# Filler products in TensorE's queue while batch 0 is being prepared

## The chip, the core and the metric

The kernel runs on one core of a Trainium2 chip. The metric is the device time of one execution in microseconds (us), as the median of several executions. A profile is taken of one execution more; it lists what every engine did, and the TensorE clock that was granted in each stretch (1.00 is 2.4 GHz, 0.50 is 1.2 GHz).

## What is computed

For each of 4 batches of 12480 rows of 128 numbers, 32 inducing rows attend to the batch (giving `h`, 32 x 128), then the batch attends to `h`, and a two-layer network with a squared ReLU follows:

```
h = mab(I, x)                      # softmax(scale * I x^T) x, 32 x 128 per batch
y = mab(x, h)                      # softmax(scale * x h^T) h, 12480 x 128 per batch
r = maximum(y @ w_in, 0)           # 128 -> 2048
out = (r * r) @ w_out              # 2048 -> 128
```

## The kernel before

Since every row of `y` is a mixture of the 32 rows of `h`, the kernel does not multiply rows by `w_in` at all. For each batch it works out, once, weights on squares of pairs of attention weights (`w16`, four blocks of 128 x 128, made from products `G_0` to `G_3`), on single squares (`side`) and a linear part (`lin`). Then it streams the batch in 26 chunks of 480 columns: `ups` makes the differences of pairs on TensorE (tile `hp`), `lifts` squares them on ScalarE (`g`), `downs` multiplies by the weights on TensorE (`po`), `evictions` and `stores` write the result.

The program has two parts. Until about 52 us it loads the weights and makes `h` of batch 0 in program order (`first`). From there on an own list scheduler, `Order`, decides the order. Each stage of the kernel is a generator that yields one operation at a time: its engine, an assumed duration, a due time and what it needs. `Order.run` keeps an assumed clock per engine; it finds the earliest possible start of any waiting operation, and of those that could start on that engine within `PATIENCE` (0.159 us) it takes the one with the earliest due time. So what is written here is an order per engine, fixed when the program is built. On the chip each engine works through its own queue in that order, waiting where an input has not come.

Between `h` of batch 0 and the first `downs` lie three strands that the prediction follows:

- `readings`: for each of 7 groups G the scores of batch 0 against `h` (L419, tile `s`, operands `xp` and `hT`; four 32-row products beside each other, fp32), read out of PSUM by VectorE (L791, tile `scored`). One PSUM tile, the ring `att`, serves all scores, so the next scores wait for VectorE's reading. `attention` makes the softmax from them on VectorE, GpSimd and ScalarE (among it L820 on VectorE and L823 on GpSimd, tile `a`) and stores it to DRAM (`ad`); `squares` loads it back as `dT`.
- `first_softmax`: the scores of batch 1 against the inducing rows (L419 again, operands `xp` and `indT_sb`), read by VectorE at L675 (tile `sT`), through the same ring `att`.
- `prepare` and `pair_weights`: the weights of batch 0. TensorE's products into the tile `bank` (L902, L948, L952, L967, L982 to L987, L1009), VectorE's steps between them (L958 to L961 on `pl`, `inc`, `hot`; L989 to L1000), VectorE's `G_0` to `G_3` (L1060), and TensorE's four blocks of pair weights (L1076, tile `wq`), each evicted by ScalarE. `mark("wq", b, c)` is set when block c has been placed in the order. The first `downs` needs the fourth block.

In the names of the orders below, `s_0_3` are the scores of batch 0, group 3 against `h`; `s_1_3` those of batch 1, group 3 against the inducing rows. The PSUM pool `ps_o` has two buffers, and the ring `po_ring` stands for them.

Of the kernel before, what the change touches and what calls it, by code (L numbers as in the profile page):

```python
# [9 lines left out]
F32 = mybir.dt.float32  # L10
# [8 lines left out]
P = 128  # L19
NB = 4  # L20
MI = 32
# [4 lines left out]
CH = 4 * TP  # L26
# [4 lines left out]
NQ = 4  # L31
# [148 lines left out]
def op(engines, took, due, *needs, alone=False, hold=None):  # L180
    return engines, took, due, needs, alone, hold
# [3 lines left out]
def attend_then_relu2_mlp(ctx: ExitStack, tc: tile.TileContext, xn, xT, indT, w_in, w_out, outT):  # L185
# [19 lines left out]
    nc = tc.nc  # L205
# [418 lines left out]
    def mark(*key):  # L624
        return marks.setdefault(key, Mark())
# [12 lines left out]
    def x_loads():  # L638

        for b in range(1, NB):  # L640
            for G, w in enumerate(WID):
                end = yield op("SP1", 3.0 * w / CH, h_due(b) - X_AT - 2.0 * (NG - G), xp_ring, alone=True, hold=HOLD)
                xp_ring.held.append(mark("read", b, G))
                sts[b].xp[G] = load_xT(b, G, flow, NX)
                mark("x", b, G).t = end

    def row_loads():

        for b in range(1, NB):
            for h in range(HALVES):  # L650
                i = h % XB
                end = yield op("SP1" if h < HALVES - 1 else "SP5", 1.5, h_due(b) - ROWS_AT + ROWS_STEP * h, xnb_free[i], alone=True, hold=HOLD)
                sts[b].rows[h] = load_half(b, h, xnb[i])
                xnb_free[i] = mark("used", b, h)
                mark("rows", b, h).t = end
# [113 lines left out]
    def readings():  # L769

        for b in range(NB):
            st = sts[b]
            for G in range(NG):
                w, t = WID[G], BLK[G]
                wb = 32 * t
                X = nominal(NCH * b + 4 * G) - 14 - SLACK
                due = X - READ_AT
                if b < NB - 1:
                    due = min(due, h_due(b + 1) - READ_UNTIL - READ_STEP * (NG - G))
                end = yield op("PE", 0.83, due, att, mark("h", b))  # L780
                done = att.take()
                ps = att_psum(f"s2_{b}_{G}")
                scores(ps, st.hT, st.xp.pop(G), w)
                mark("read", b, G).t = end
                end = yield op("DVE", 0.62, due + 1, slots)
                gone = slots.take()
                k = 480 * ((NG * b + G) % SLOTS)
                e = scored[:, k:k + 480].rearrange("p (t i) -> p t i", i=MI)
                if wb > w:
                    nc.vector.memset(ps[:, w:wb], 0.0)  # L790
                nc.vector.transpose(e.rearrange("p t i -> p (t i)")[:, 0:wb], ps[:, 0:wb])  # L791
                done.t = end
                order.add(attention(b, G, e, X, end, gone))

    def attention(b, G, e, X, since, gone):
# [40 lines left out]
        done.t = end  # L836
        mark("ad", b, G).t = end

    def squares():

        for b in range(NB):
            st = sts[b]
            for G, n in enumerate(GRP):
                X = nominal(NCH * b + 4 * G) - 11 - SLACK
                rows = slice(0, MI * n)
                end = yield op("SP3", 1.4, X, mark("ad", b, G), dT_ring, alone=True)
                dT_ring.held.append(mark("over", b, G))
                dT = st.aT[G] = load_dT(b, G)
                mark("dT", b, G).t = end
                order.add(square(b, G, n, X, rows, dT))  # L850
# [236 lines left out]
    def ups():  # L1087

        for n, (b, c) in enumerate(CHUNKS):
            st = sts[b]  # L1090
            for j in (0, 1):
                end = yield op("PE", 0.21, nominal(n - 1.5 + UP_STEP * j), hp_ring, mark("dT", b, c // 4), alone=True)
                hp_ring.held.append(mark("lifted", n, j))
                dT = st.aT[c // 4][:, :, (c % 4) * TP:(c % 4 + 1) * TP]
                hp = hps[n, j] = two_banks(f"hp_{b}_{c}_{j}")
                for i in range(2):
                    nc.tensor.matmul(  # L1097
                        hp[:, i, 0:CH].rearrange("p (q t) -> p q t", q=4), pairs[half(i), (2 * j + i) * P:(2 * j + i + 1) * P],
                        dT[half(i)], start=True, stop=True,
                    )  # L1100
                mark("up", n, j).t = end

    def lifts():

        for n, (b, c) in enumerate(CHUNKS):
            for j in (0, 1):
                end = yield op("ACT", 0.92, nominal(n - 1 + j / 2), mark("up", n, j), *([] if j else [g_ring]), alone=True)
                if j == 0:
                    g_ring.held.append(mark("down", n))
                    gs[n] = mlp.tile([P, NQ, CH], F16, tag="g", name=f"g_{b}_{c}")  # L1110
                nc.scalar.activation(gs[n][:, 2 * j:2 * j + 2], hps.pop((n, j))[:, 0:2, 0:CH], AF.Square)  # L1111
                mark("lifted", n, j).t = end
            mark("g", n).t = end

    def downs():

        for n, (b, c) in enumerate(CHUNKS):
            st = sts[b]
            needs = [mark("g", n), mark("zz", b, c // 4), mark("wq", b), mark("lin", b), po_ring]
            end = yield op("PE", 1.12, nominal(n + 0.8), *needs, alone=True)  # L1120
            po_ring.held.append(mark("out", n))
            dT = st.aT[c // 4][:, :, (c % 4) * TP:(c % 4 + 1) * TP]
            po = pos_[n] = ps_o.tile([P, 512], F32, tag="po", name=f"po_{b}_{c}")
            g = gs.pop(n)
            r = slice(32 * (c % 4), 32 * (c % 4) + 32)
            zz = st.zz[c // 4][r].rearrange("p q t -> p (q t)")
            nc.tensor.matmul(po[:, 0:CH], st.side[r], zz, start=True, stop=False)  # L1127
            for i in range(NQ):
                nc.tensor.matmul(po[:, 0:CH], st.w16[:, i], g[:, i], start=False, stop=False)  # L1129
            nc.tensor.matmul(po[:, 0:CH].rearrange("p (q t) -> p q t", q=4), st.lin[0:96], dT[0:96], start=False, stop=True)  # L1130
            mark("down", n).t = end
            if c == NCH - 1 or c % 4 == 3:
                mark("over", b, c // 4).t = end
            if n == len(CHUNKS) - 4:
                tc.mark_branch_hint_location("whole", engines=[E.PE, E.Activation, E.DVE, E.SP])

    def evictions():

        for n, (b, c) in enumerate(CHUNKS):
            st = sts[b]  # L1140
            end = yield op("ACT|DVE" if n < len(CHUNKS) - 1 else "ACT", 0.7, nominal(n + 1.1), mark("down", n), o_ring, alone=True)
            o_ring.held.append(mark("stored", n))
            o = outs[n] = work.tile([P, CH], F32, tag="o", name=f"o_{b}_{c}", bufs=NO)
            po = pos_.pop(n)
            if order.chosen == "ACT":
                nc.scalar.activation(o, po[:, 0:CH], AF.Identity, bias=st.bias, scale=st.osc)  # L1146
            else:
                nc.vector.tensor_scalar(o, po[:, 0:CH], st.osc, st.bias, op0=ALU.mult, op1=ALU.add)  # L1148
            mark("out", n).t = end

    def stores():

        for n, (b, c) in enumerate(CHUNKS):
            end = yield op("SP1", 0.69, nominal(n + 1.5), mark("out", n), alone=True)
            nc.sync.dma_start(outT[:, b, c], outs.pop(n))
            mark("stored", n).t = end

    def smallest():

        needs = [mark("ad", NB - 1, G) for G in range(NG)]  # L1160
        yield op("DVE", 0.2, nominal(NCH * NB - 10), *needs)
        m = small("dmin")
        nc.vector.tensor_reduce(m, least_d.rearrange("p b g -> p (b g)"), axis=AX.X, op=ALU.min)
        yield op("PE", 0.15, nominal(NCH * NB - 10), mark("checked", NB - 1))
        tp = side_psum("dmin_t")
        nc.tensor.transpose(tp[0:1, 0:P], m, ident)
        yield op("DVE", 0.4, nominal(NCH * NB - 10))
        t = work.tile([1, 1], F32, tag="dmin1", name="dmin1")
        nc.vector.tensor_reduce(t, tp[0:1, 0:P], axis=AX.X, op=ALU.min)
        nc.vector.tensor_scalar(flags[:, NB:NB + 1], t, D_MIN, None, op0=ALU.is_ge)  # L1170

    prepare_w_out()
    for st in sts[1:]:
        st.rows = {}
    for job in (ups(), lifts(), downs(), evictions(), stores(), readings(), squares(), x_loads(), row_loads(), first_softmax(), smallest()):
        order.add(job)
    for b in range(NB):
        order.add(prepare(b))
# [194 lines left out]
```

## Time and profile before

| what | value |
|---|---|
| median of 3 executions | 392.14 us (390.17 to 392.18) |
| the profiled execution | 394.02 us, of it 392.2 us from the first to the last instruction |
| TensorE products busy | 340.5 us (87% of the span) |
| VectorE busy | 325.1 us (83%) |
| ScalarE busy | 274.2 us (70%) |
| GpSimd busy | 137.6 us (35%) |
| mean granted TensorE clock | 0.960 |
| DMA | 91.12 MB, mean 232 GB/s |

The profiled execution took 1.88 us more than the median of the three. Busy time says how long an engine had an instruction in it, not whether anybody waited for it; the rows further below give for single instructions the start, the duration, and in brackets the idle time of the engine just before and what ended it.

### The profile page before, as it was taken

To read this page: it belongs to the slowest core of one execution; us is meant where nothing else is said; L and a number is where in the kernel's file an instruction comes from. 1 tells how busy PE (TensorE), PEld (TensorE's weight loads), DVE (VectorE), ACT (ScalarE), POOL (GpSimd) and SP (SyncE) were. 2 spreads that over 40 slices of the span, in tenths; PEclk is the share of its full clock that TensorE was granted. 3 is DMA by queue.
4 is the path that set the end of the run, shared out by engine and by line. 5 is a ranking of instruction groups with operands and counts; after the bars stand their busy time and mean duration, and the time that the engine had idled before them with its cause. 6 is when DMAs were issued, how large, how long until landed. Compare 5 with 4: busy or idle time off the path is not lost.

```text
span 392.2 us, 9162 instructions
## 1 busy us (share of the span) xinstructions
PE 340.5 (87%) x3373; PEld 148.6 (38%) x3373; DVE 325.1 (83%) x863; ACT 274.2 (70%) x382; POOL 137.6 (35%) x149
## 2 busy tenths in 40 slices
PE   0893674886998998998899999999999999999993
PEld 0652530435533324444332334453433544333331
DVE  8959979779897898899688989978999899976531
ACT  1463360147596796698787886897889989898983
POOL 1000013223574432256374323374555136744000
PEclk9998797686999999999999999999999999999998
DMA  7984139933998987989989898888763444475432
GB/s 260 417 281 125 55 124 373 299 105 96 330 295 235 302 249 278 309 291 296 299 276 320 271 324 289 274 279 283 234 202 120 166 139 132 168 256 164 147 125 104
DMA packets 48786, 91.12 MB, mean 232 GB/s; under 512 B 7905, under 2 KB 38881, under 8 KB 48737
## 3 DMA queue, kind: packets, MB, share of 16 engines
q1 hardware_dynamic: 48736, 90.49, 69.4%
q8 instruction: 27, 0.44, 0.5%
q14 instruction: 23, 0.18, 0.2%
HBM read 58.52 MB, written 31.95 MB: 231 GB/s over the span
## 4 chain that ended last, share of the span: by engine, by line
PE 37%; DVE 7%; ACT 4%; DMA 4%; issue 1%; SPq 0%; ACTq 0%; DVEq 0%
PE po L1129 14%; PE hp L1097 8%; PE s L419 4%; ACT g L1111 3%; PE po L1130 3%; DMA xnb<-xn_dram 3%; PE po L1127 2%; PE hacc L744 2%; PE wq L1076 2%; DVE o L1148 1%; DVE G L1060 1%; PE sq L859 1%; DVE sT L675 1%; DMA outT_dram<-o 1%; PE bank L1009 1%
## 5 line engine op out<-in xcount | busy, mean ns | idle before, releaser
L1111 ACT ACTIVATE g<-hp 128x960 f16<-128x960 f32 x208 | 191.7, 971 | 51.3 <-PE hp L1097 47.8
L1129 PE MATMUL po<-g,w 128*128 128x480 f16 x416 | 102.3, 369 | 0.0
L1148 DVE TENSOR_SCALAR o<-po,osc,bias 128x480 f32<-128x480 f32 x72 | 55.0, 765 | 25.3 <-PE po L1130 23.9
L1097 PE MATMUL hp<-dT,pairs 32*128 32x480 f16 x416 | 67.9, 368 | 3.4 <-ACT g L1111 3.2
L1129 PEld LDWEIGHTS <-w 128*128 128x128 f16 x416 | 32.2, 97 | 57.9 <-issue 36.0
L807 POOL TENSOR_TENSOR scored<-scored,mx 128x480 f32<-128x480 f32 (+1 forms) x28 | 26.2, 940 | 75.4 <-DVE mx L805 73.2
L816 POOL TENSOR_TENSOR scored<-scored,z 128x480 f32<-128x480 f32 (+1 forms) x28 | 26.5, 947 | 55.4 <-DVE z L814 40.7
L873 POOL TENSOR_TENSOR zz<-z 128x480 f16<-128x480 f32 (+1 forms) x28 | 28.8, 1029 | 45.9 <-DVE z L867 40.7
L833 POOL TENSOR_TENSOR a<-a,a 128x480 f16<-128x480 f32 (+1 forms) x28 | 28.9, 1035 | 37.6 <-DVE a L827 25.4
L1127 PE MATMUL po<-zz,side 32*128 32x480 f16 x104 | 38.2, 367 | 0.8 <-DVE o L1148 0.6
L1097 PEld LDWEIGHTS <-pairs 32*128 32x128 f16 x416 | 17.1, 92 | 55.9 <-issue 53.6
L1130 PE MATMUL po<-dT,lin 96*128 96x480 f16 x104 | 38.2, 367 | 0.0
L419 PE MATMUL s<-xp,indT_sb 128*32 128x480 f32 (+1 forms) x224 | 29.0, 591 | 6.6 <-DMA xp<-xT_dram 1.8
L823 POOL TENSOR_TENSOR a<-a,lessen 128x480 f32<-128x480 f32 (+1 forms) x28 | 27.3, 975 | 21.0 <-DVE a L820 20.8
L419 PE MATMUL s<-xp,hT 128*32 128x480 f32 (+1 forms) x224 | 27.6, 565 | 5.0 <-DVE scored L791 4.1
L1060 DVE TENSOR_TENSOR G<-hwp,hw 128x512 f16<-128x512 f16 x64 | 28.8, 509 | 0.0
L744 PE MATMUL hacc<-xnb,en 128*32 128x128 f32 x588 | 25.5, 288 | 3.5 <-DMA xnb<-xn_dram 3.1
L1146 ACT ACTIVATE o<-po,bias,osc 128x480 f32<-128x480 f32 x32 | 24.0, 758 | 5.4 <-PE po L1130 4.4
L444 ACT COPY xp<-xt 128x896 f32<-128x896 f32 (+1 forms) x13 | 12.3, 957 | 17.4 <-PE xt L441 17.4
L809 ACT ACTIVATE scored<-scored 128x480 f32<-128x480 f32 (+1 forms) x28 | 16.0, 576 | 11.9 <-POOL scored L807 11.8
L791 DVE STREAM_TRANSPOSE scored<-s 128x480 f32<-128x480 f32 (+1 forms) x28 | 18.1, 646 | 5.1 <-PE s L419 4.6
L744 PEld LDWEIGHTS hacc<-xnb,en 128*32 128x32 f32 x588 | 16.3, 114 | 14.3 <-issue 6.3
(231 smaller groups left out, 487.3 us busy)
## 6 DMA issues: line engine op xcount, KB each, us to landing
outT_dram<-o SPq DMA_DIRECT2D x104, 240.0 KB, 3.1
xp<-xT_dram SPq DMA_DIRECT2D x18, 960.0 KB, 7.5
xnb<-xn_dram SPq DMA_DIRECT2D x21, 512.0 KB, 5.6
xnb<-xn_dram SPq DMA_DIRECT2D x23, 448.0 KB, 5.4
dT<-ad SPq DMA_DIRECT2D x72, 120.0 KB, 3.4
ad<-a SPq DMA_DIRECT2D x24, 240.0 KB, 3.5
wi<-w_in_dram SPq DMA_DIRECT2D x4, 512.0 KB, 5.9
wo<-w_out_dram SPq DMA_DIRECT2D x16, 128.0 KB, 3.4
```

The lines of the kernel that those rows point to most:

```text
L419: nc.tensor.matmul(ps[32 * q:32 * q + 32, 0:w], lhsT, xp[:, w * q:w * q + w], start=True, stop=True,)
L744: nc.tensor.matmul(hacc[32 * q:32 * q + 32, 0:P], st.en[G][:, t], xg[:, t % 8], start=G == 0 and t < 4, stop=G == NG - 1 and t + 4 >= nb32,)
L823: nc.gpsimd.tensor_tensor(a[:, 0:w], a[:, 0:w], lessen.broadcast_to([P, w]), op=ALU.add)
L833: nc.gpsimd.tensor_tensor(a16[:, 1, 0:w], a[:, 0:w], a16[:, 0, 0:w], op=ALU.subtract)
L873: nc.gpsimd.tensor_tensor(g[rows], zv[rows], zv[rows], op=ALU.mult)
L1060: nc.vector.tensor_tensor(g[:, :, MI * j:MI * j + n], hwp[:, :, 0:n], hw16f[:, :, s0:s0 + n], op=ALU.mult)
L1097: nc.tensor.matmul(hp[:, i, 0:CH].rearrange("p (q t) -> p q t", q=4), pairs[half(i), (2 * j + i) * P:(2 * j + i + 1) * P], dT[half(i)], st ...
L1111: nc.scalar.activation(gs[n][:, 2 * j:2 * j + 2], hps.pop((n, j))[:, 0:2, 0:CH], AF.Square)
L1127: nc.tensor.matmul(po[:, 0:CH], st.side[r], zz, start=True, stop=False)
L1129: nc.tensor.matmul(po[:, 0:CH], st.w16[:, i], g[:, i], start=False, stop=False)
L1130: nc.tensor.matmul(po[:, 0:CH].rearrange("p (q t) -> p q t", q=4), st.lin[0:96], dT[0:96], start=False, stop=True)
L1148: nc.vector.tensor_scalar(o, po[:, 0:CH], st.osc, st.bias, op0=ALU.mult, op1=ALU.add)
```

## The change

A new job, `filler`, is added first to the scheduler's list. As long as the third block of batch 0's pair weights has not been placed, it offers TensorE one product of the constant `pairs` with itself (a 128 x 32 weight, 480 columns, fp16) at any time, with an assumed duration of 0.2 us and a due time later than any other. The result goes to a PSUM tile that nobody reads. It holds one of the two `po` buffers until the last filler.

```
+    def filler():
+
+        done = po_ring.take()
+        ps = ps_o.tile([P, 512], F32, tag="po", name="filler")
+        while mark("wq", 0, NQ - 2).t is None:
+            end = yield op("PE", 0.2, 1e9, alone=True)
+            nc.tensor.matmul(ps[0:MI, 0:CH], pairs[:, 0:MI], pairs[:, 0:CH], start=True, stop=True)
+        done.t = end
...
-    for job in (ups(), lifts(), downs(), evictions(), stores(), readings(), squares(), x_loads(), row_loads(), first_softmax(), smallest()):
+    for job in (filler(), ups(), lifts(), downs(), evictions(), stores(), readings(), squares(), x_loads(), row_loads(), first_softmax(), smallest()):
```

It places 66 fillers, each with a load of its weight, at 17 places of TensorE's order: 37 of them ahead of `s_1_0`, 28 from there to the third block `wq`, and one just behind that block. Lines from 839 on stand 9 lines further down in the changed file. The orders of ScalarE, GpSimd and the DMA queue are the same as before.

TensorE's order from the second scores of batch 0 to the first of batch 1, before:

```order
L419 MATMUL s_0_1_663<-xp_1_266,hT_161 32x480 x4
L902 MATMUL bank_678<-ssq,every 128x1
L419 MATMUL s_0_2_681<-xp_2_292,hT_161 32x480 x4
L419 MATMUL s_0_3_702<-xp_3_328,hT_161 32x480 x4
L419 MATMUL s_0_4_725<-xp_4_354,hT_161 32x480 x4
L419 MATMUL s_0_5_745<-xp_5_400,hT_161 32x480 x4
L419 MATMUL s_0_6_753<-xp_6_426,hT_161 32x240 x4
L419 MATMUL s_1_0_767<-xp_0_659,indT_sb 32x480 x4
```

The same place of TensorE's order in the change, its beginning:

```order
L419 MATMUL s_0_1_662<-xp_1_266,hT_161 32x480 x4
L845 LDWEIGHTS pairs
L845 MATMUL filler<-pairs 32x480
...
L911 MATMUL bank_682<-ssq,every 128x1
...
L419 MATMUL s_0_2_687<-xp_2_292,hT_161 32x480 x4
...
L419 MATMUL s_0_3_714<-xp_3_328,hT_161 32x480 x4
```

Three fillers stand behind `s_0_1`, two behind the product into `bank`, then 6, 10, 5, 6 and 5 behind `s_0_2` to `s_0_6`; nothing else has moved here.

TensorE's order around the fourth scores of batch 1, before (L1009 is 64 products):

```order
L987 MATMUL bank_678<-onec,cat_137 128x1
L1009 LDWEIGHTS g_0_811
L1009 MATMUL bank_678<-w_hi,g_0_811 32x128
...
L419 MATMUL s_1_3_935<-xp_3_743,indT_sb 32x480 x4
L419 MATMUL s_1_4_952<-xp_4_762,indT_sb 32x480 x4
```

The same place of TensorE's order in the change (L1018 is L1009 of before):

```order
L996 MATMUL bank_682<-onec,cat_137 128x1
L845 LDWEIGHTS pairs
L845 MATMUL filler<-pairs 32x480
...
L419 MATMUL s_1_3_914<-xp_3_775,indT_sb 32x480 x4
L1018 LDWEIGHTS g_0_849
L1018 MATMUL bank_682<-w_hi,g_0_849 32x128
...
L419 MATMUL s_1_4_989<-xp_4_796,indT_sb 32x480 x4
```

Three fillers come in, and the scores `s_1_3` have moved ahead of the 64 products.

VectorE's order at the first pair products `G_0`, before:

```order
L1000 TENSOR_SCALAR tsg<-sgn,t 128x4
L820 STREAM_TRANSPOSE a_0_1_942<-scored 128x480
L675 TENSOR_SCALAR sT_797,mx_643<-s_1_3_935 128x480
L1060 TENSOR_TENSOR G_0_946<-hwp_724,hw_0_709 128x16x32 x4
L675 TENSOR_SCALAR sT_797,mx_643<-s_1_4_952 128x480
```

The same place of VectorE's order in the change:

```order
L1009 TENSOR_SCALAR tsg<-sgn,t 128x4
L675 TENSOR_SCALAR sT_835,mx_644<-s_1_3_914 128x480
L820 STREAM_TRANSPOSE a_0_1_987<-scored 128x480
L1069 TENSOR_TENSOR G_0_994<-hwp_746,hw_0_721 128x16x32 x4
L675 TENSOR_SCALAR sT_835,mx_644<-s_1_4_989 128x480
```

The reading of `s_1_3` and the transpose into `a` have changed places; that is the only difference in VectorE's order. Behind the third block `wq`, TensorE's `sq_1` (L859) has also moved behind the second half of the first row sums (L744).

## Rows read from the trace of the kernel before

**Rows 1.** Stretches of the span: busy us of each engine (instructions), clock, DMA share, GB/s.

```profile
55.70:64.00 8.30, 3.94 (x34) 0.93 (x34) 7.65 (x23) 2.51 (x5) 2.92 (x3) 1.00 0.93 340
64.00:74.20 10.20, 7.93 (x88) 3.13 (x84) 6.87 (x22) 1.30 (x3) 2.09 (x2) 0.50 0.97 341
74.20:77.80 3.60, 2.32 (x44) 1.44 (x37) 3.39 (x16) 0.00 (x0) 0.95 (x1) 0.97 1.04 303
77.80:81.10 3.30, 2.98 (x72) 1.87 (x71) 1.58 (x8) 0.00 (x0) 1.03 (x2) 0.50 0.70 279
81.10:91.30 10.20, 7.96 (x83) 3.39 (x79) 9.56 (x33) 6.58 (x9) 2.09 (x2) 1.00 0.39 113
91.30:98.10 6.80, 4.60 (x65) 3.89 (x68) 6.80 (x13) 4.91 (x15) 3.32 (x3) 0.50 0.11 23
110.00:390.00 280.00, 266.12 (x2481) 105.55 (x2479) 232.76 (x595) 229.51 (x309) 117.00 (x121) 1.00 0.72 237
```

**Rows 2.** Timeline of VectorE from 60 to 100 us: start, us, instruction, idle before.

```profile
65.09 0.68 DVE L791 STREAM_TRANSPOSE scored<-s 128x480 f32<-128x480 f32 x1 [0.60 <-PE s L419]
...
70.22 0.66 DVE L675 TENSOR_SCALAR_CACHE_REDUCE sT<-s 128x480 f32<-128x480 f32 x1 [0.83 <-PE s L419]
...
72.64 0.16 DVE L958 COPY pl<-bank 128x1 f32<-128x1 f32 x1 [1.16 <-PE bank L952]
...
74.25 0.66 DVE L675 TENSOR_SCALAR_CACHE_REDUCE sT<-s 128x480 f32<-128x480 f32 x1 [0.66 <-PE s L419]
...
78.81 0.67 DVE L820 STREAM_TRANSPOSE a<-scored 128x480 f32<-128x480 f32 x1
81.50 0.66 DVE L675 TENSOR_SCALAR_CACHE_REDUCE sT<-s 128x480 f32<-128x480 f32 x1 [2.02 <-PE s L419]
...
82.09 1.46 DVE L1060 TENSOR_TENSOR G<-hwp,hw 128x512 f16<-128x512 f16 x4
...
95.84 2.46 DVE L1060 TENSOR_TENSOR G<-hwp,hw 128x512 f16<-128x512 f16 x4
98.23 0.28 DVE L1062 CAST G<-hwS 128x256 f16<-128x256 f32 x1
```

**Rows 3.** Timeline of TensorE from 59 to 99 us.

```profile
59.03 1.01 PE L419 MATMUL s<-xp,hT 128*32 128x480 f32 x8 [0.81 <-DVE scored L791]
61.78 1.01 PE L419 MATMUL s<-xp,hT 128*32 128x480 f32 x8 [1.74 <-DVE scored L791]
63.60 1.44 PE L419 MATMUL s<-xp,hT 128*32 128x480 f32 x8 [0.80 <-DVE scored L791]
...
68.33 1.83 PE L419 MATMUL s<-xp,indT_sb 128*32 128x480 f32 x8 [1.48 <-issue]
...
70.64 1.92 PE L952 MATMUL bank<-wo_sb,hwS 128*32 128x128 f32 x30
...
78.12 1.90 PE L1009 MATMUL bank<-w_hi,g 128*32 128x128 f16 x64 [1.14 <-DVE off L994]
79.78 1.65 PE L419 MATMUL s<-xp,indT_sb 128*32 128x480 f32 x8
...
98.83 1.07 PE L1076 MATMUL wq<-w_hi,G 128*128 128x128 f16 x16
```

**Rows 4.** Chain of work that ended last, later batches: start, us, what.

```profile
188.60 0.92 PE po L1129 x4
...
307.37 0.93 PE bank L952 x31
```

**Rows 5.** Timeline of GpSimd from 75 to 100 us.

```profile
79.56 0.98 POOL L823 TENSOR_TENSOR a<-a,lessen 128x480 f32<-128x480 f32 x1 [1.72 <-DVE a L820]
...
95.34 0.99 POOL L823 TENSOR_TENSOR a<-a,lessen 128x480 f32<-128x480 f32 x1 [2.75 <-DVE a L820]
```

**Rows 6.** Timeline of the DMA queue, then DMA issues from 71 to 73 us.

```profile
71.08 1.28 SPq L566 DMA_DIRECT2D dT<-ad  x3
...
dT<-ad SPq DMA_DIRECT2D x3, 120.0 KB, 5.6
```

**Rows 7.** Who waited for whom on TensorE, 98 to 392 us: total, times, longest.

```profile
PE hacc L744 <- DMA xnb<-xn_dram: 3.1, 3, 1.6
```

## The prediction

> **What bounds the kernel now.** I read the stretches first. From 110 to 390 us TensorE is busy for 266.12 of 280 us at a granted clock of 1.00 [rows 1]: that part is bound by TensorE, and products without use would only harm it; none is placed there. The fillers lie between 55 and about 93 us, where the clock falls to 0.50 three times: from 64.0 to 74.2, from 77.8 to 81.1 and from 91.3 to 98.1 us, 20.3 us together [rows 1]. So the second thing to read is who waits in these stretches. VectorE is busy for 7.65 of the 8.30 us before the first fall and for 9.56 of 10.2 us between 81.1 and 91.3 us, but only for 6.87 of 10.2 and 1.58 of 3.30 us in the first two slow stretches [rows 1]. The timeline of VectorE says why: it stands idle for 0.60, 0.83, 1.16, 0.66 and 2.02 us, each time until TensorE has finished scores or L952 [rows 2]. From 82.09 us, the start of G_0, it has next to no idle time until G_3 ends at 98.51 us (98.23 + 0.28) [rows 2], and the fourth block wq, for which the first downs wait, starts at 98.83 us [rows 3]. The preparation is thus a VectorE chain with five holes that TensorE makes, at half its clock in most of them. What can be won lies in these holes; a slow product that VectorE does not wait for is worth nothing.
>
> **What half the clock costs.** Scores of 480 columns take 1.01 us at a clock of 1.00 and 1.83 us at 0.50 [rows 3]; L952 takes 1.92 us at 0.50 [rows 3] and 0.93 in a later batch [rows 4].
>
> **What a filler costs.** No row shows one. Four fp16 products of 480 columns advance the chain by 0.92 us, 0.23 each, at full clock [rows 4]; L952's ratio 1.92/0.93 makes that 0.47 at half clock. I take 0.23, since the clock is 1.00 where the fillers begin [rows 1]. The bounds are nothing (a filler that only fills idle time) and 0.47.
>
> **Whether the clock holds.** Before the first fall TensorE was busy for 3.94 of 8.30 us [rows 1], with idle stretches of 0.81, 1.74 and 0.80 us between the scores [rows 3]. The fillers are put into exactly these, so that it would be busy nearly throughout. It also fell after 7.96 busy us of 10.2, and rose in a stretch with 7.93 [rows 1], so busy time alone does not order the cases, and no row shows a product that uses a quarter of the array's columns by itself. I take it that the clock holds at 1.00 and keep the other case as a rival.
>
> **The sum, along VectorE's chain.** In each step a positive number is later than before.
>
> Ahead of s_0_4 stand 10 fillers, 2.30 us, where the idle time was 1.74 us [rows 3], and 6 fillers (1.38 against 0.81) have already delayed s_0_3 by some 0.7, of which VectorE's own work hid a part. By issue order s_0_4 starts at about 63.0 instead of 61.78, and its reading comes 1.2 later. The 5 fillers behind it (1.15 against 0.80) push s_0_5 to 65.05; it then takes 1.01 instead of 1.44, so its reading comes at about 66.1 instead of 65.09: **+1.0**. This is the price of the fillers.
>
> s_1_0 starts at about 69.3 instead of 68.33 and takes 1.01 instead of 1.83. VectorE, itself 1.0 late, no longer waits the 0.83 us there: +0.2. L952 in 0.95 instead of 1.92 removes 1.1 of the 1.16 us before L958: **-0.9**. s_1_1 at full clock removes 0.62 of the 0.66 before the next L675: **-1.55**.
>
> Then comes the largest hole, 2.02 us [rows 2]. Before, s_1_3 stood behind the 64 products of L1009, which wait for L994 and take 1.90 us at half clock; then s_1_3 took 1.65 [rows 3]. Now s_1_3 stands ahead of them, behind three fillers (0.7 us, in the 1.14 us that TensorE idled there), and is ready before VectorE has finished L1000. VectorE does L675 and L820, whose order is exchanged at no cost, without a gap, and G_0 starts 1.9 earlier still: **-3.45**.
>
> One thing is given back. L820 now stands right before G_0, and it releases L823 on GpSimd, which before ran alone at 79.56 while VectorE idled [rows 5]. With GpSimd idle the four instructions of G_0 took 1.46 us; G_3, at 95.84 with L823 running from 95.34 [rows 5], took 2.46 for four of the same [rows 2]. I take half of that 1.0, since L823 (0.98 us) covers part of G_0 alone: +0.5, bounds 0 and 1.0. G_0 ends **2.95** earlier.
>
> From there VectorE works without a gap, and its order is the same, so G_1 to G_3 follow. The other fillers (3, 2, 1, 5, 9 and single ones) stand where TensorE waits for ScalarE or VectorE; the 9 before the third block, 2.1 us, lie in the time of G_2. They cost nothing as long as VectorE is the later one; if it gets faster, they become the wait. The fourth block started 0.32 after G_3's end, behind row sums at half clock; at full clock these end in time, 0.25 more. So the first downs start about **3.2 us earlier**.
>
> What could be late instead is the transfer of dT, which sq_0 needs: issued from 71.08, landed 5.6 later, at 76.7 to 78 [rows 6]. TensorE now wants it at about 79, so it is hidden with 1 us to spare. The DMA share was 0.39 and 0.11 from 81.1 to 98.1 us [rows 1], which leaves room for stores and loads that come earlier.
>
> Behind that point the same work stands in the same order, each load issued by what it waited for before, so I carry the 3.2 us to the end: 394.02 would become 390.8 for a profiled execution. That one lies 1.88 above the median, 392.14, from which I forecast **388.9**.
>
> **The likeliest case's own range.** Fillers that cost nothing give 1.0 more, no help from GpSimd's overlap 0.5 more; the whole 1.0 of the overlap and 0.5 of further delays take 1.0 away. With a spread of runs of about 1 us that is 386.8 to 390.4.
>
> **Rivals.**
>
> *The gain is not carried on.* The rest waits for loads in places: 3.1 us in row sums alone [rows 7]. If loads of a later batch are held by something that the shift doesn't move, those waits grow by what was won: 391.0 to 392.1. Against it: all loads behind 86 us are issued behind work that has shifted. Chance 0.17.
>
> *The clock falls at 64 us all the same*, because a narrow product does not count for the clock; this is the case that ends slower. The mechanism is TensorE's queue order: from s_0_5 on the fillers take 0.47 and stand ahead of the scores that VectorE waits for. 5 fillers push s_0_5 to 66.3, where it takes 1.44; 6 (2.8 us) push s_0_6 to 70.5, ending 71.5; 5 (2.35) push s_1_0 to 73.7, against 68.33: +5.4. Five more before L1009 add 1.2 where 1.1 was idle, and s_1_3 ahead of L1009 gives about 1.4 back. Some 4.0 later: 396.1. It decides at the point where the 16 fillers from s_0_4 to s_1_0 cost over half a microsecond each more than the idle time they fill. Chance 0.12.
>
> *All the slow time comes back.* TensorE was busy for 7.93, 2.98 and 4.60 us at half clock [rows 1], 15.5 together; if each were on the path, half of it, 7.75, would return: 384.4. Against it: VectorE is busy for 6.80 of the 6.80 us of the third stretch [rows 1]. Chance 0.04. (The Trainium skill, "TensorE: Matmul & The Clock Gate", section Terms, goes further: the penalty is about the throttled time times the share of pulses withheld. By that, an estimate from this page, the 20.3 us would give 10.15 back, and the time would be 382.0. The rows above disagree, since they show who waited.)
>
> *Little of it was there.* One execution before took 390.17, so the falls of the clock may be fewer in unprofiled runs than in the profile; then half of the gain is left, 390.6. Chance 0.07.
>
> **How the numbers follow.** The forecast has 0.60. A measurement tells a change of over 0.5%, 1.96 us, from none, so faster means below 390.18. That takes 0.55 of the forecast's 0.60, the 0.04 of the third rival and a little of the first: 0.60. The same: 0.15 of the first rival, 0.07 of the last, 0.05 of the forecast: 0.27. Slower: 0.13. The range, 386.6 to 392.8, takes in the likeliest case and the first and last rivals; it leaves out the slow and the largest case (0.16) and some of the tails.
>
> **What would show it.** In the profile after: the granted clock at 1.00 from 55 to 100 us; VectorE's holes before L958 and the L675 rows gone, and one of about 1 us before the L791 of s_0_5 or s_0_4; G_0 starting near 78.6 and the fourth block near 95.6. I would be wrong if the clock is 0.50 somewhere from 64 to 80 us, if the first downs come as late as before, or if they come early while a wait for a load later on has grown.

## The result and the profile after

| | before | with the change |
|---|---|---|
| median, us | 392.16 (390.17 to 393.87, 4 executions) | 386.91 (385.52 to 388.07, 4 executions) |
| profiled execution, us | 394.02 | 386.45 |
| its span, us | 392.2 | 384.7 |
| mean granted clock | 0.960 | 0.986 |

The ratio is 0.9897, 95% interval 0.9848 to 0.9946: faster by 1.0%, about 4.0 us. In a second, larger set (12 executions of the change against 23 of the kernel before) it was 0.9912 (0.9875 to 0.9949). Medians here take all executions, ratios only undisturbed ones, so the two need not agree to the last tenth.

The stretches of the span, as in [rows 1] (busy us of TensorE, its weight loads, VectorE, ScalarE, GpSimd, then the clock, DMA share and GB/s):

```profile
55.70:64.00 8.30, 7.87 (x56) 3.35 (x56) 6.97 (x21) 2.51 (x5) 2.60 (x3) 1.00 0.94 341
64.00:74.20 10.20, 9.31 (x129) 4.45 (x128) 9.69 (x34) 1.30 (x3) 2.09 (x2) 1.00 0.97 334
74.20:77.80 3.60, 3.57 (x87) 2.11 (x90) 3.44 (x18) 0.00 (x0) 1.05 (x2) 1.00 1.00 332
77.80:81.10 3.30, 2.81 (x25) 0.67 (x17) 3.30 (x9) 1.83 (x2) 1.10 (x2) 1.00 0.62 241
81.10:91.30 10.20, 10.05 (x104) 5.33 (x104) 9.71 (x29) 8.17 (x17) 3.02 (x3) 1.00 0.41 115
91.30:98.10 6.80, 5.18 (x116) 3.85 (x105) 6.80 (x14) 1.94 (x8) 3.54 (x4) 1.00 0.72 243
```

The three falls of the clock are gone, and VectorE, which was busy for 6.87 of 10.2 us and 1.58 of 3.30 us in the first two slow stretches, now is for 9.69 and 3.30. TensorE's timeline with the fillers, answering to [rows 3]:

```profile
60.14 1.99 PE L845 MATMUL filler<-pairs 128*32 128x480 f16 x9
61.86 0.60 PE L419 MATMUL s<-xp,hT 128*32 128x480 f32 x3
...
63.96 1.01 PE L419 MATMUL s<-xp,hT 128*32 128x480 f32 x8
...
68.28 1.01 PE L419 MATMUL s<-xp,indT_sb 128*32 128x480 f32 x8 [0.70 <-issue]
...
69.56 1.07 PE L961 MATMUL bank<-wo_sb,hwS 128*32 128x128 f32 x30
...
74.89 1.11 PE L419 MATMUL s<-xp,indT_sb 128*32 128x480 f32 x8
75.73 1.18 PE L1018 MATMUL bank<-w_hi,g 128*32 128x128 f16 x64
...
94.98 1.07 PE L1085 MATMUL wq<-w_hi,G 128*128 128x128 f16 x16 [1.62 <-DVE G L1071]
...
96.99 0.37 PE L1136 MATMUL po<-zz,side 32*128 32x480 f16 x1
```

The products of the kernel take what they take at full clock (scores 1.01 us; L961, which is L952 of before, 1.07; the row at 61.86 us holds only the first three products of `s_0_4`). A row of nine fillers spans 1.99 us, of which 0.37 is the duration of the last one, so the starts lie 1.62/8 = 0.20 us apart. And at the end TensorE waits for VectorE (1.62 us before the fourth block), no longer the other way round. VectorE's timeline, answering to [rows 2]:

```profile
63.22 0.68 DVE L791 STREAM_TRANSPOSE scored<-s 128x480 f32<-128x480 f32 x1 [0.46 <-PE s L419]
...
65.03 0.68 DVE L791 STREAM_TRANSPOSE scored<-s 128x480 f32<-128x480 f32 x1 [0.25 <-PE s L419]
...
69.35 0.66 DVE L675 TENSOR_SCALAR_CACHE_REDUCE sT<-s 128x480 f32<-128x480 f32 x1
...
70.92 0.15 DVE L967 COPY pl<-bank 128x1 f32<-128x1 f32 x1
...
71.78 0.64 DVE L675 TENSOR_SCALAR_CACHE_REDUCE sT<-s 128x480 f32<-128x480 f32 x1
...
76.42 0.65 DVE L675 TENSOR_SCALAR_CACHE_REDUCE sT<-s 128x480 f32<-128x480 f32 x1
...
77.59 2.22 DVE L1069 TENSOR_TENSOR G<-hwp,hw 128x512 f16<-128x512 f16 x4
```

The four large holes carry no wait any more; of the fifth, 0.60 us before the L791 of `s_0_5`, 0.25 are left. G_0 starts at 77.59 instead of 82.09, and takes 2.22 us instead of 1.46. GpSimd runs L823 beside it:

```profile
77.75 1.09 POOL L823 TENSOR_TENSOR a<-a,lessen 128x480 f32<-128x480 f32 x1 [2.29 <-DVE a L820]
```

All further runs are read by two measures from their profiles. The *stretch* goes from the first scores of batch 0 (L419) to the first product of the downs (L1127); TensorE and VectorE wait for no load in it (except 0.6 us with double fillers), and it repeats to 0.1 us. The *tail* goes from there to the end of the span.

| kernel | first scores | first downs | stretch | tail |
|---|---|---|---|---|
| before | 53.06 | 100.84 | 47.78 | 291.4 |
| before, again | 52.97 | 100.65 | 47.68 | 288.2 |
| change | 52.74 | 96.99 | 44.25 | 287.7 |
| change, again | 53.02 | 97.27 | 44.25 | 288.4 |
| order alone | 52.88 | 100.02 | 47.14 | 287.6 |
| fillers in the old order | 52.35 | 97.07 | 44.72 | 287.8 |
| fillers stop early | 52.51 | 96.60 | 44.10 | 289.4 |
| half fillers | 52.98 | 96.58 | 43.61 | 297.5 |
| half fillers, again | 52.39 | 95.99 | 43.60 | 287.9 |
| half fillers, stop early | 53.45 | 97.81 | 44.35 | 289.2 |
| the same, L820 later | 53.19 | 97.00 | 43.81 | 289.9 |
| half fillers throughout, L820 later | 52.41 | 95.30 | 42.89 | 286.8 |
| fillers of 32 rows | 52.45 | 108.31 | 55.87 | 294.2 |
| double fillers | 52.41 | 106.11 | 53.69 | 288.3 |

So of the 7.5 us between the two first profiles, 0.3 lie ahead of the first scores, 3.5 in the stretch, and 3.7 in the tail.

### The profile page after: what moved, and what is told of

Same layout as the page of the kernel before. It is cut to its first block, busy times and chain, and to the rows that moved or that the text cites. A ratio compares the mean times of both kernels' runs of the same rounds, so it can differ in the third digit from the quotient of the medians.

```text
span 384.7 us, 9294 instructions
## 1 busy us (share of the span) xinstructions
PE 345.5 (90%) x3439; PEld 151.1 (39%) x3439; DVE 325.4 (85%) x863; ACT 274.2 (71%) x382; POOL 137.5 (36%) x149
## 4 chain that ended last, share of the span: by engine, by line
PE 60%; DVE 16%; DMA 11%; ACT 7%; issue 3%; SPq 1%; POOL 1%; ACTq 0%; DVEq 0%
PE po L1138 18%; PE hp L1106 10%; PE s L419 9%; DMA xnb<-xn_dram 7%; ACT g L1120 4%; PE po L1139 4%; DMA xp<-xT_dram 4%; PE hacc L744 4%; PE po L1136 3%; PE wq L1085 3%; DVE G L1069 3%; PE xt L441 2%; PE filler L845 2%; PE sq L868 1%; DVE sT L675 1%
## 5 line engine op out<-in xcount | busy, mean ns | idle before, releaser
L816 POOL TENSOR_TENSOR scored<-scored,z 128x480 f32<-128x480 f32 (+1 forms) x28 | 26.3, 940 | 51.8 <-DVE z L814 43.3
L823 POOL TENSOR_TENSOR a<-a,lessen 128x480 f32<-128x480 f32 (+1 forms) x28 | 27.4, 980 | 22.3 <-DVE a L820 22.1
L419 PE MATMUL s<-xp,indT_sb 128*32 128x480 f32 (+1 forms) x224 | 27.0, 548 | 3.3 <-DVE sT L458 0.9
L419 PE MATMUL s<-xp,hT 128*32 128x480 f32 (+1 forms) x224 | 27.7, 548 | 0.9 <-DVE hT L520 0.9
L744 PE MATMUL hacc<-xnb,en 128*32 128x128 f32 x588 | 24.5, 278 | 2.7 <-DMA xnb<-xn_dram 2.7
L791 DVE STREAM_TRANSPOSE scored<-s 128x480 f32<-128x480 f32 (+1 forms) x28 | 18.1, 646 | 5.6 <-PE s L419 5.0
L876 DVE TENSOR_SCALAR z<-sq,off,cut 128x480 f32<-128x480 f32 (+1 forms) x28 | 21.2, 756 | 0.0
```

Source lines behind the costliest of these rows:

```text
L419: nc.tensor.matmul(ps[32 * q:32 * q + 32, 0:w], lhsT, xp[:, w * q:w * q + w], start=True, stop=True,)
L744: nc.tensor.matmul(hacc[32 * q:32 * q + 32, 0:P], st.en[G][:, t], xg[:, t % 8], start=G == 0 and t < 4, stop=G == NG - 1 and t + 4 >= nb32,)
L823: nc.gpsimd.tensor_tensor(a[:, 0:w], a[:, 0:w], lessen.broadcast_to([P, w]), op=ALU.add)
```

## The experiments

**Order alone.** No product is placed, only its time is reserved:

```
-            nc.tensor.matmul(ps[0:MI, 0:CH], pairs[:, 0:MI], pairs[:, 0:CH], start=True, stop=True)
```

> The scheduler reserves the fillers' time as in the change but places no product, so the order of all engines is that of the change and the 66 fillers are missing. Measure: the stretch from the first scores of batch 0 (L419) to the first product of the downs, 47.78 us before and 44.25 in the change. Theory (the clock and the holes that TensorE made): the clock falls to 0.50 near 64 us as before; only the hole before the reading of s_1_3 shrinks, since L1009 no longer stands ahead of it (up to 1.9 us), and 0.5 to 0.8 is given back by GpSimd beside G_0; 46.3 to 47.0, time 390.5 to 392. Rival (the moved scores did it, not the clock): 44.0 to 44.6, time as in the change.

Ratio 0.9972 (0.9942 to 1.0002), stretch 47.14: 0.64 less than before, a little short of what was expected, far from the change. Two stretches of this kernel:

```profile
63.70:73.80 10.10, 7.84 (x68) 2.72 (x60) 6.99 (x23) 0.96 (x3) 2.08 (x2) 0.50 0.93 331
...
83.90:87.20 3.30, 3.07 (x27) 1.73 (x24) 3.20 (x12) 1.83 (x2) 1.58 (x2) 0.52 0.46 122
```

and VectorE in it:

```profile
70.39 0.66 DVE L675 TENSOR_SCALAR_CACHE_REDUCE sT<-s 128x480 f32<-128x480 f32 x1 [0.83 <-PE s L419]
...
72.81 0.16 DVE L965 COPY pl<-bank 128x1 f32<-128x1 f32 x1 [1.15 <-PE bank L959]
...
74.20 0.66 DVE L675 TENSOR_SCALAR_CACHE_REDUCE sT<-s 128x480 f32<-128x480 f32 x1 [0.45 <-PE s L419]
...
79.95 2.21 DVE L1067 TENSOR_TENSOR G<-hwp,hw 128x512 f16<-128x512 f16 x4
```

The clock falls at 63.7 us as before, and three of the holes stay, with 0.83, 1.15 and 0.45 us (0.83, 1.16 and 0.66 before). The fourth, 2.02 us, has gone with the moved scores alone; but G_0 takes 2.21 us instead of 1.46, and a fall at 83.9 us and a wait of VectorE for ScalarE (0.57 us, at 89.4) eat more of it.

**Fillers in the old order.** A table writes 65 of the fillers in at their places, and the scheduler knows nothing of them:

```
+TABLE = {("ssq", 0): 3, ("s2", 0, 2): 2, ("s2", 0, 3): 6, ("s2", 0, 4): 10, ("s2", 0, 5): 5, ("s2", 0, 6): 6, ("s1", 1, 0): 5,
+         ("hot", 0): 2, ("g4", 0): 3, ("s1", 1, 4): 1, ("sq", 0, 0): 2, ("s1", 1, 5): 3, ("hp", 1, 1): 2, ("s1", 1, 6): 1,
+         ("hp", 3, 0): 5, ("wq", 0, 2): 9}
...
+                fill("s2", b, G)
                 scores(ps, st.hT, st.xp.pop(G), w)
```

> 65 of the fillers are written in at their places by a table, and everything else keeps the order of before: L1009 ahead of s_1_3, L820 ahead of L675 on VectorE. Theory (clock): granted clock 1.00 from 52 to 97 us, L1009 and s_1_3 take about 1.1 and 1.0 us instead of 1.90 and 1.65, G_0 runs without GpSimd in 1.5 us; stretch 44.0 to 44.8. Rival (the moved scores did it): the fillers' delay of about 0.5 to 1 us alone is left, 47.5 to 48.8.

Ratio 0.9929 (0.9901 to 0.9957), stretch 44.72, 3.06 less than before, clock 1.00 throughout:

```profile
52.00:97.00 45.00, 40.34 (x508) 19.91 (x508) 40.06 (x121) 17.36 (x34) 12.49 (x13) 1.00 0.72 246
```

VectorE, in the order of before:

```profile
77.28 0.66 DVE L681 TENSOR_SCALAR_CACHE_REDUCE sT<-s 128x480 f32<-128x480 f32 x1 [0.58 <-PE s L424]
...
77.86 1.46 DVE L1081 TENSOR_TENSOR G<-hwp,hw 128x512 f16<-128x512 f16 x4
```

With s_1_3 still behind L1009 the hole of 2.02 us shrinks to 0.58 without any move, and G_0, with no GpSimd instruction beside it, keeps its 1.46. The products bring 3.06 of the 3.53 us, the moved order 0.64 by itself; the two overlap in that hole.

**The kernel before, again.**

> The kernel before, unchanged, for a second profile. From the first product of the downs to the end of the span the profile before took 291.4 us and that of the change 287.7. If this difference of 3.7 us is luck of the two profiles (waits for loads), the second profile lies anywhere from 287 to 291.5 and the stretch ahead of the downs stays at 47.5 to 48.1. If the change brings it, the second profile is again at 291 to 292.

Ratio 0.9991 (0.9951 to 1.0031). The stretch repeats (47.68), the tail does not: 288.2 against 291.4. The waits of TensorE for loads from 97 to 300 us (total, times, longest), first profile:

```profile
PE hacc L744 <- DMA xnb<-xn_dram: 3.1, 3, 1.6
PE s L419 <- DMA xp<-xT_dram: 1.8, 2, 1.5
PE sq L859 <- DMA dT<-ad: 1.1, 1, 1.1
```

and the second:

```profile
PE hacc L744 <- DMA xnb<-xn_dram: 3.6, 3, 2.3
PE s L419 <- DMA xp<-xT_dram: 0.9, 1, 0.9
```

The change's own profile lists 2.7, 0.3 and 0.2 us for the three. All the kernels have the same work behind the first downs. Their tails lie between 286.8 and 291.4 us, apart from one of 294.2 and one of 297.5, and not in the order of the stretches. So most of the 3.7 us is how one execution went; that the change has some share in it can't be excluded by profiles that scatter by 3 us and more. The larger set's 3.4 us (2.0 to 4.9) is no more than the 3.5 us of the stretch, so by that set the share is at most some 1.4 us.

**Fillers stop early.** 14 of the 66, at the last places, are left out:

```
-        while mark("wq", 0, NQ - 2).t is None:
+        while mark("wq", 0, 0).t is None:
```

> The fillers end with the first block of pair weights instead of the third: 52 are left, the 5, 9 and 1 behind it are gone. Theory of the prediction (the third slow stretch is hidden under VectorE and worth only 0.25 us): the clock falls to 0.50 once between 86 and 95 us, the stretch from first scores to first downs is 44.2 to 44.6 us, the time that of the change. Rival (the late fillers carry part of the gain): 45.2 us or more.

Ratio 0.9910 (0.9867 to 0.9953), stretch 44.10, a little under the range of the theory, and the clock fell once:

```profile
89.80:93.20 3.40, 3.40 (x48) 2.85 (x50) 3.40 (x6) 2.56 (x9) 1.83 (x2) 0.50 0.00 0
```

This fall lasted 3.4 us and was hidden under VectorE: the fourth block still waited for it. The run with half fillers that stop early, below, shows that this need not be so.

**Half fillers.**

```
-            nc.tensor.matmul(ps[0:MI, 0:CH], pairs[:, 0:MI], pairs[:, 0:CH], start=True, stop=True)
+            nc.tensor.matmul(ps[0:MI, 0:CH // 2], pairs[:, 0:MI], pairs[:, 0:CH // 2], start=True, stop=True)
```

> Every filler has 240 columns instead of 480, at the same places, so it takes about 0.10 us instead of 0.20. If the fillers' time in the queue is a price and the clock still holds: the scores of batch 1 come 0.2 to 0.3 us earlier than in the change, and the stretch from first scores to first downs is 43.8 to 44.1 us (44.25 in the change). If half as much filling lets the clock fall near 64 us: scores and L952 take 1.83 and 1.92 us again and the stretch is 45.5 to 47 us.

Ratio 0.9892 (0.9836 to 0.9947), stretch 43.61. The clock stays at 1.00, and the scores of batch 1 start 15.06 us after the first scores instead of 15.54, more than was expected: the price of the fillers is real, and in this run the clock held with half of the filling. The other 0.16 us lie where VectorE's L698 waited 0.26 us in the change for L695, which stands behind five fillers; with half fillers that wait is gone, and a longer G_2 gives 0.13 of it back. The tail of 297.5 us holds a wait for a load, and behind it the clock was at half for some 10 us:

```profile
180.59 1.08 PE L744 MATMUL hacc<-xnb,en 128*32 128x128 f32 x16 [2.08 <-DMA xnb<-xn_dram]
```

```profile
180.00:190.00 10.00, 9.41 (x58) 3.04 (x59) 4.19 (x12) 4.75 (x5) 3.03 (x3) 0.51 0.76 269
```

The same kernel once more:

> The half fillers throughout once more, for a second set of executions and a second profile. Stretch 43.5 to 43.7 us again, ratio 0.987 to 0.991, a little under that of the change (0.9897 and 0.9912); from the first downs to the end 287 to 290 us, if the 297.5 of the first profile was a wait for loads of that execution alone.

Ratio 0.9927 (0.9891 to 0.9963), a little above the expected 0.987 to 0.991; stretch 43.60, tail 287.9. The 0.64 us are below what these ratios can tell; only the stretch shows them.

**Double fillers.**

```
+            for _ in range(2):
                 nc.tensor.matmul(ps[0:MI, 0:CH], pairs[:, 0:MI], pairs[:, 0:CH], start=True, stop=True)
```

> Two products at each of the 66 places, the scheduler assuming 0.2 us for both together. Theory (a filler stands in TensorE's queue ahead of scores that VectorE waits for, 0.2 us each): the idle time ahead of s_1_0 is filled already, so 37 more fillers push the scores of batch 1 by 5 to 6 us, and the stretch becomes 50 to 53 us, the time 394 to 396. Rival (fillers are free as long as the clock is up): stretch below 46.

Ratio 1.0144 (1.0068 to 1.0220), stretch 53.69, median 396.84. At full clock all the way the kernel is slower than before: s_1_0 comes 5.7 us later than in the change, as expected, and another 3.7 come behind it, 0.6 of them a wait for a load, so that the stretch is longer than expected. One of its rows, 19 fillers ahead of `s_0_4`:

```profile
61.54 4.01 PE L846 MATMUL filler<-pairs 128*32 128x480 f16 x19
```

66 more fillers, 13.2 us at 0.20, cost 8.8 beside the load: of a second helping two thirds are on the path.

**Fillers of 32 rows.**

```
-            nc.tensor.matmul(ps[0:MI, 0:CH], pairs[:, 0:MI], pairs[:, 0:CH], start=True, stop=True)
+            nc.tensor.matmul(ps[0:MI, 0:CH], pairs[0:32, 0:MI], pairs[0:32, 0:CH], start=True, stop=True)
```

> The fillers use 32 rows of the array instead of 128 (32 x 32 weights), at the same places and with the same columns. If any product in the queue holds the clock, all is as in the change: clock 1.00 from 52 to 97 us, stretch 44.0 to 44.5. If the clock asks how much of the array works: 0.50 in part of 60 to 80 us, fillers of 0.4 us, and the stretch grows to 46 to 52 us.

The stretch grew to 55.87 us, beyond the range expected. The profile's stretches:

```profile
55.00:58.60 3.60, 3.29 (x22) 1.04 (x19) 2.69 (x8) 2.30 (x5) 1.00 (x1) 1.00 0.95 356
58.60:82.20 23.60, 23.60 (x115) 6.71 (x112) 11.83 (x37) 1.12 (x3) 4.07 (x4) 0.50 0.71 238
```

and TensorE in it:

```profile
60.00 1.83 PE L419 MATMUL s<-xp,hT 128*32 128x480 f32 x8
61.76 4.18 PE L845 MATMUL filler<-pairs 32*32 32x480 f16 x10
```

TensorE was busy for all of 23.60 us and ran at 0.50 in all of them. Ten fillers took 4.18 us; at 0.20 us from start to start and 0.37 for the last they would take some 2.2. This is the mechanism of the prediction's slow rival, slow fillers ahead of the scores that VectorE waits for, only earlier (from 58.6 us instead of 64) and bigger: the stretch is 8.1 us longer than before, the rival had 4.0. It did not happen each time: of 11 executions six took 388.2 to 390.7 us at a mean clock of 0.983 to 0.989, five 397.2 to 404.4 us at 0.946 to 0.957. The ratio, 0.9963 (0.9920 to 1.0006), is that of the six alone.

**Half fillers, stop early.** Both edits together:

> Fillers of 240 columns that end with the first block of pair weights (52 are left). If price and cover are as the runs so far say, both savings hold together: clock 1.00 until about 88 us, the stretch from first scores to first downs 43.4 to 43.7 us (44.25 in the change, 43.61 with half fillers throughout), ratio to before 0.986 to 0.991. If half fillers hold the clock only by the density of those that are now left out, the clock falls before 85 us and the stretch is 44.5 or more.

Ratio 0.9951 (0.9916 to 0.9986), stretch 44.35: the savings do not hold together. TensorE at the end of the stretch:

```profile
90.08 1.89 PE L1085 MATMUL wq<-w_hi,G 128*128 128x128 f16 x16 [2.20 <-ACT sT L710]
...
93.15 2.72 PE L744 MATMUL hacc<-xnb,en 128*32 128x128 f32 x44
95.80 1.07 PE L1085 MATMUL wq<-w_hi,G 128*128 128x128 f16 x16
```

The third block comes behind a hole of 2.20 us, in which nine of the fillers that are left out would stand (with them, in the run with half fillers throughout, 1.17 us of the hole are left and the clock holds). In this hole the clock fell, and it stayed at 0.50 from 88.8 to 95.6 us, twice as long as with full fillers that stop early. The third block took 1.89 us, and the row sums (L744) behind it kept the fourth block waiting. It began 1.03 us after the last pair product of G_3, where with half fillers throughout it was 0.26: the late fillers are worth 0.8 us when the fall comes at this place.

**L820 later, to take GpSimd away from G_0**, on top of the last two edits:

```
-        end = yield op("DVE", 0.62, X - 1.8, a32_ring)
+        end = yield op("DVE", 0.62, X - (1.4 if (b, G) == (0, 1) else 1.8), a32_ring)
```

> As half_stop, and VectorE's L820 of group 1 is due 0.4 us later, which puts it behind G_0 and so takes GpSimd's L823 away from G_0. If GpSimd beside it is what makes G_0 2.2 us instead of 1.46: G_0 takes 1.45 to 1.6 us, and the stretch is 42.8 to 43.3 us. If G_0 is slow for another reason, it stays at 2.0 to 2.3 us. The order behind it changes too (a store of batch 0 and the third pair products move), so part of it can be given back.

Ratio 0.9954 (0.9926 to 0.9983), stretch 43.81. G_0 took 1.46 us, as expected; the stretch did not reach its range; the clock fell at the same place as in the run before, 0.50 from 88.4 to 94.8 us. So the early stop was taken back:

> Half fillers up to the third block as in half_fill, with L820 of group 1 behind G_0 as in half_late. If the late fillers keep the clock, and with it the row sums ahead of the fourth block, off the path: clock 1.00 from 52 to 97 us, stretch 42.6 to 43.1 us (43.81 in half_late, 43.61 in half_fill). If the row sums wait for VectorE's L827 whatever the clock: 43.5 or more.

Ratio 0.9851 (0.9803 to 0.9899), stretch 42.89, median 384.54: faster than the kernel before by 1.5%. Against the change it was not timed side by side; its stretch is 1.36 us shorter. (The order behind L820 moves too, and 64 fillers are placed instead of 66.) VectorE's pair products in it:

```profile
76.17 1.46 DVE L1069 TENSOR_TENSOR G<-hwp,hw 128x512 f16<-128x512 f16 x4
...
83.60 1.45 DVE L1069 TENSOR_TENSOR G<-hwp,hw 128x512 f16<-128x512 f16 x4
...
86.09 2.19 DVE L1069 TENSOR_TENSOR G<-hwp,hw 128x512 f16<-128x512 f16 x4
...
90.57 2.46 DVE L1069 TENSOR_TENSOR G<-hwp,hw 128x512 f16<-128x512 f16 x4
```

GpSimd beside them:

```profile
78.88 0.99 POOL L823 TENSOR_TENSOR a<-a,lessen 128x480 f32<-128x480 f32 x1 [4.24 <-DVE a L820]
...
82.60 1.00 POOL L807 TENSOR_TENSOR scored<-scored,mx 128x480 f32<-128x480 f32 x1
86.31 1.00 POOL L816 TENSOR_TENSOR scored<-scored,z 128x480 f32<-128x480 f32 x1 [2.72 <-DVE z L814]
90.06 0.99 POOL L823 TENSOR_TENSOR a<-a,lessen 128x480 f32<-128x480 f32 x1 [2.75 <-DVE a L820]
91.01 1.19 POOL L882 TENSOR_TENSOR zz<-z 128x480 f16<-128x480 f32 x1
```

G_0 and G_1 lie beside no GpSimd instruction and take 1.46 and 1.45 us; G_2 meets L816 and G_3 two of them, and they take 2.19 and 2.46.

**The change, again.**

> The change, unchanged, timed over more executions. Theory: stretch 44.1 to 44.4 us again, since nothing in it waits for a load; the waits for loads behind the first downs differ from profile to profile by a microsecond or two. The ratio to the kernel before lies at 0.988 to 0.992, which is 3.5 us and a little.

Ratio 0.9912 (0.9875 to 0.9949), stretch 44.25, the same to the hundredth.

## Why the prediction was right

It forecast 388.9 us, 3.2 us less than before. Measured were 386.91: 5.2 less by the two medians of four executions, 3.4 to 4.0 by the two ratios, and 3.5 in the stretch. So 386.91 stands 2.0 under the forecast and close to the lower end of the range. Much of that is luck of few executions: the larger set has 387.54 against 391.39, 3.9 less. The terms below together gave 0.3 more than forecast. The step from the profile to the median, 1.88 us, lay in the tail and was luck of that profile, as the second one shows.

- *The bound*, a VectorE chain with holes that TensorE makes: right. Four of the five holes were closed, and the fourth block now waits 1.62 us for VectorE.
- *The clock holds*: right, and this, not the moved order, is what brings most of the gain (3.06 of 3.53 us with the order of before). Most slow products had nobody waiting for them. By the rule of the Trainium skill that the prediction cites ("TensorE: Matmul & The Clock Gate", Terms) 10.15 us would have come back, an estimate from that page. The trace disagrees with it: 3.5 came.
- *The price of the fillers*, +1.0 us at the reading of s_0_5: the term that was mis-sized. Counted from the first scores the reading came at 12.29 us instead of 12.03, only +0.26. A filler costs 0.20 us, not the 0.23 that the prediction took from four downs in the chain, and it lies under the end of the product before; `s_0_4` was 0.4 late, not 1.2. VectorE waits 0.46 us for it and 0.25 for `s_0_5`, where one wait of about 1 us was expected. This is where the change did better than forecast: L675 of s_1_0 stood at -0.55 instead of +0.2, G_0's start at -4.2 instead of -3.45.
- *GpSimd beside G_0*, +0.5: the sign was right and the size was 0.76 (2.22 against 1.46), shown by moving L820 away. The prediction took half of the 1.0 us that G_3 had lost before and put that to L823 alone. But G_3 lay beside L823 for only 0.49 us, and beside a second instruction of GpSimd for 1.18. The nearer row was G_1, beside one instruction, 0.56 us longer than G_0. G_1 and, of GpSimd, the instruction beside it and the second one beside G_3, in the kernel before:

```profile
87.73 2.02 DVE L1060 TENSOR_TENSOR G<-hwp,hw 128x512 f16<-128x512 f16 x4
```

```profile
87.44 0.99 POOL L807 TENSOR_TENSOR scored<-scored,mx 128x480 f32<-128x480 f32 x1 [1.57 <-DVE mx L805]
...
96.28 1.18 POOL L873 TENSOR_TENSOR zz<-z 128x480 f16<-128x480 f32 x1
```

- *The third slow stretch is worth 0.25*: 0.26 came in the change, but 0.8 hung on it in the run with half fillers that stop early. So 0.25 is not its price in every case, and the fillers there insure against the rest.
- *Carried to the end*: the tails of the two profiles of the change (287.7 and 288.4 us) are no longer than those before (291.4 and 288.2), and the ratios show 3.4 to 4.0 us. That excludes the first rival. How much of the tail's own 3.7 us belongs to the change stays open.
- *The slow rival*: it did not come in the profiles with fillers of 128 rows. With 32 rows the one profile shows it, and five of 11 executions have such a time and clock.

## What to carry to other kernels

Where an engine runs at half clock, look for who waits in the slow stretches before pricing them: with the order of before, 20.3 us at half clock were worth 3.1 us here. Filler products pay where they fill only idle time of the queue. Each stands ahead of the next real product, so try short ones first: 240 columns on 128 rows held the clock here and cost less, 480 columns on 32 rows did not hold it in five of 11 executions. Be careful with stopping early: leaving out the last 14 saved 0.15 us with long fillers and cost 0.7 to 0.9 with short ones. When a gap closes, look at what now runs beside the next instruction: a free GpSimd had made G_0 fast before.

## What was not expected of the hardware

TensorE ran at 0.50 for 23.6 us in which it was busy all the time, with 32-row products between the scores, where 128-row products in the same places and of the same length held 1.00; why a part of the executions escaped it was not tried, and stays open. Fillers of half the length held it too, with TensorE busy for 26.88 of 33.0 us from 55 to 88 us in the run that stops early. And four pair products on VectorE take 1.46 us alone, 2.0 to 2.3 beside one GpSimd instruction of 1.0 to 1.2 us, 2.46 beside two.
